# A fixed order for the last token tile, and its output stored in two halves

## The chip, the cores and the metric

The kernel runs on one core of a Trainium2 chip. The core has a matrix engine (TensorE, PE in the profile, with its weight loads under PEld), a vector engine (VectorE, DVE), an activation engine (ScalarE, ACT), GpSimd (POOL) and a sync engine (SyncE, SP) that here only starts transfers. The engines run beside one another, each in its own order, and wait for one another by semaphores. The metric is the device time of one execution in microseconds; the kernel before has a median of 182.74 us in 4 runs (181.94 to 183.9).

## The reference

The computation is attention over 8 heads with a local window of 96 positions and 8 global ones, and behind it a mixing block whose input is the attention's output. With batch 4, sequence 768, model width 512:

```
x  = attention(q, k, v)                    # (4, 768, 512)
theta = x @ w_theta
zr, zi = x * cos(theta), x * sin(theta)
y  = w_tok_r @ zr + w_tok_i @ zi           # over the 768 positions
u  = x + y
out = u + max(u @ w_ch, 0)
```

The change touches only the last two lines, for the last 128 positions of the last batch.

## The kernel before, in words

Positions are cut into NT = 6 tiles of T = 128. Each of the 4 batches goes through three stages.

**Attention** (`prep`, `scores`, `values`) leaves x in `x_sb`. **theta** makes the angles, their cosine and sine, and the products `zri`. **The mixing block**, which is what matters here, has three steps for a tile `tt`:

- `mix(b, tt, g)`, g = 0 to 2: four matmuls each (L377), 12 in all, that add up y for the tile in one PSUM buffer. Behind the last one VectorE adds x and writes `u` (L382).
- `utrans(b, tt)`: turns `u` into `uT`, with the channels on the partitions. In batches 1 to 3 that is a transfer with transpose on SP's queue (L391), except for the very last tile, (3, 5). That one is turned by four TensorE transposes (L395) and a copy out of PSUM on ScalarE (L396).
- `chan(b, tt)`: four matmuls of `uT` with `w_ch` (L402), the activation and sum on VectorE into `o_sb` (L405), and a store of 256 KB on SP's queue (L407).

The program emits the steps of a batch in a list, `main`, and `chan` lags three tiles behind `mix`. In the last batch there is no further attention to weave in, so the list itself is what is emitted. Its end for tiles 4 and 5 is: mix(4,0), chan(1), mix(4,1), mix(4,2), utrans(4), mix(5,0), chan(2), mix(5,1), mix(5,2), utrans(5). The three `chan` steps that are left over, 3 to 5, are in `rest` (L565) and are emitted behind the loop (L568). The first part of the program has an order written out by hand (`manual_schedule`, L83, closed at L528); what follows it is ordered by the scheduler of the language, bound to lie behind the last instruction of that part on PE, DVE and ACT (`fences`). For the end of the last batch the built program's order on PE is the order of emission.

Small PSUM tiles (`ps`) come from a pool of four, taken in turn by `mix`, `utrans` and `chan`; `uT` has 5 buffers, `u` 6 and `o_sb` 4.

Of the kernel before, what the change touches and what calls it, by code (L numbers as in the profile page):

```python
# [12 lines left out]
ALU = mybir.AluOpType  # L13
# [3 lines left out]
def kernel(  # L17
# [13 lines left out]
    nc = tc.nc  # L31
    B, H, S, D = q.shape
    T = 128
    NT = S // T
    DM = H * D
# [20 lines left out]
    def ps_small(shape, dtype):  # L56
        return small.tile(shape, dtype, name="ps", tag="ps")
# [30 lines left out]
    for i_, eng in ((1, nc.sync), (0, nc.scalar)):  # L88
        eng.dma_start(out=qk32[:, i_].rearrange("p h t d -> p h (t d)"),
                      in_=(q, k)[i_][0, 0:2].rearrange("h (p t) d -> p h (t d)", p=T))  # L90
# [62 lines left out]
    def trans_w(tt, copy=nc.vector.tensor_copy):  # L153
        for wi in range(2):
            ps = ps_small([T, NT, T], BF)
            for st in range(NT):
                nc.tensor.transpose(ps[:, st, :], w_nat[wi, tt][:, st * T:(st + 1) * T], ident)
            (copy if wi else nc.vector.tensor_copy)(out=w_tokT[wi][:, :, tt * T:(tt + 1) * T], in_=ps)  # L158
# [50 lines left out]
    def prep(b, p):  # L209
        qk = loads[b][0]  # L210
        if (b, 0) not in qkT:
            alloc_x(b)

        qkn = att.tile([T, NT, 2, 2, D], BF, name="qkn", bufs=3)
        with behind("dve"):
            for i_ in range(2):
                nc.vector.tensor_copy(  # L217
                    out=qkn[:, :, i_].rearrange("p t h d -> p h t d"), in_=qk[:, i_, 2 * p:2 * p + 2])
        qT = att.tile([T, S], BF, name="qT", bufs=6)
        kT = att.tile([T, S], BF, name="kT", bufs=6)  # L220
        for i_, dst in ((0, qT), (1, kT)):
            ps = ps_small([T, NT, T], BF)
            with behind("pe"):
                for t_ in range(NT):
                    nc.tensor.transpose(ps[:, t_, :], qkn[:, t_, i_].rearrange("p h d -> p (h d)"), ident)  # L225

            dst = dst.rearrange("p (n t) -> p n t", t=NT)
            src = ps.rearrange("p t n -> p n t")
            if i_ == 0:
                nc.vector.tensor_copy(out=dst, in_=src)  # L230
            else:
                nc.scalar.copy(out=dst, in_=src)  # L232

        qkT[(b, p)] = [qT, kT, None]
        kglob(b, p)
# [113 lines left out]
    def theta(b, c, j):  # L349
        if c == 0 and j == 0:  # L350
            zri[b] = moe.tile([T, 2, NT, DM], BF, name="zri", tag="zri", bufs=1)
        xT, xb = xT_sb[b], x_sb[b]
        if j == 0:
            pss["th"] = ps_big()
        pb = pss["th"]
        st = 2 * c + j
        for dc in range(NC):
            nc.tensor.matmul(pb[:, j, :], lhsT=xT[:, dc, st * T:(st + 1) * T],  # L358
                             rhs=w_theta_bf[:, dc, :], start=(dc == 0), stop=(dc == NC - 1))
        if j == 1:  # L360
            cs = moe.tile([T, 2, 2, DM], BF, name="cs")
            nc.scalar.activation(cs[:, 0], pb, AF.Sin, bias=halfpi)  # L362
            ins = nc.scalar.activation(cs[:, 1], pb, AF.Sin).ins  # L363
            for i_ in range(2):
                for j_ in range(2):
                    nc.vector.tensor_mul(  # L366
                        zri[b][:, i_, 2 * c + j_, :].rearrange("p (g d) -> p g d", g=NP),
                        xb[:, :, 2 * c + j_, :],
                        cs[:, i_, j_].rearrange("p (g d) -> p g d", g=NP))

    def mix(b, tt, g):
        if g == 0:
            pss["mix"] = ps_small([T, DM], FP)
        ps = pss["mix"]
        for st in (2 * g, 2 * g + 1):
            for wi in range(2):
                anchor["pe"] = nc.tensor.matmul(  # L377
                    ps, lhsT=w_tokT[wi][:, st, tt * T:(tt + 1) * T], rhs=zri[b][:, wi, st, :],
                    start=(st == 0 and wi == 0), stop=(st == NT - 1 and wi == 1)).ins
        if g == NT // 2 - 1:  # L380
            u_sb[b, tt] = moe.tile([T, DM], BF, name="u", bufs=6)
            anchor["dve"] = nc.vector.tensor_add(  # L382
                u_sb[b, tt].rearrange("p (g d) -> p g d", g=NP), x_sb[b][:, :, tt, :],
                ps.rearrange("p (g d) -> p g d", g=NP)).ins

    def utrans(b, tt):
        u = u_sb[b, tt]
        uT = moe.tile([T, NC, T], BF, name="uT", bufs=5)
        uTs[(b, tt)] = uT
        if b and (b, tt) != (B - 1, NT - 1):  # L390
            nc.sync.dma_start_transpose(out=uT, in_=u)  # L391
            return
        ps = ps_small([T, NC, T], BF)
        for dc in range(NC):
            nc.tensor.transpose(ps[:, dc, :], u[:, dc * T:(dc + 1) * T], ident)  # L395
        nc.scalar.copy(out=uT, in_=ps)  # L396

    def chan(b, tt):
        u, uT = u_sb[b, tt], uTs[(b, tt)]
        ps_c = ps_small([T, DM], FP)  # L400
        for dc in range(NC):
            nc.tensor.matmul(ps_c, lhsT=uT[:, dc, :], rhs=w_ch_bf[:, dc, :],  # L402
                             start=(dc == 0), stop=(dc == NC - 1))
        o_sb = moe.tile([T, DM], FP, name="o_sb", bufs=4)
        nc.vector.scalar_tensor_tensor(o_sb, in0=ps_c, scalar=0.0, in1=u,  # L405
                                       op0=ALU.max, op1=ALU.add)
        nc.sync.dma_start(out=out[b, tt * T:(tt + 1) * T, :], in_=o_sb)  # L407

    def load_all(b):
        alloc_loads(b)  # L410
        load_qk(b, 0, 8)
        load_v(b, 0, 8)
# [4 lines left out]
    def load_piece(b, i):  # L417
        if i == 0:
            alloc_loads(b)
        g = nc.gpsimd.tensor_copy(out=gates[:, i:i + 1], in_=uTs[b - 2, i][0:1, 0, 0:1]).ins  # L420
        with tc.issue_after(g):
            if i < H // 2:
                load_qk(b, 2 * i, 2)
            else:
                load_v(b, (i - H // 2) * (H // 2), H // 2)
# [17 lines left out]
    def weave(main, side, s0=0.0, s1=1.0):  # L443

        total = float(sum(w for w, _ in main)) or 1.0
        stot = float(sum(w for w, _ in side)) or 1.0
        done, sdone, i_ = 0.0, 0.0, 0
        for w, f in main:
            f()
            done += w  # L450
            while i_ < len(side) and s0 + (s1 - s0) * (sdone + side[i_][0] / 2) / stot <= done / total:
                side[i_][1]()
                sdone += side[i_][0]
                i_ += 1
        while i_ < len(side):
            side[i_][1]()
            i_ += 1
# [74 lines left out]
    rest = []  # L532
    for b in range(B):
        nxt = b + 1 if b + 1 < B else None
        if b == 0:
            load_all(2)
        lag = 3
        th = [lambda c=c, j=j: theta(b, c, j) for c in range(NT // 2) for j in range(2)]
        pre = [lambda p=p: prep(nxt, p) for p in range(NP)] if nxt else []
        if b == 0:  # L540
            order = []
        elif nxt:
            order = rest[:-1] + pre[:2] + th[:2] + pre[2:] + th[2:3] + rest[-1:] + th[3:]
        else:
            order = rest[:-1] + th[:3] + rest[-1:] + th[3:]
        for f in order:
            f()
        main = []
        for tt in range(NT):
            for g in range(NT // 2):  # L550
                main.append((2048, lambda tt=tt, g=g: mix(b, tt, g)))
                if b == 0 and g == 1 and tt + 1 < NT:
                    main.append((1536, lambda tt=tt: trans_w(tt + 1)))
                if tt >= lag and g == 0:
                    main.append((2048, lambda tt=tt: chan(b, tt - lag)))
                if b == 0 and tt and g == 1:
                    main.append((512, lambda tt=tt: utrans(b, tt - 1)))
            if b:
                main.append((0, lambda tt=tt: utrans(b, tt)))
            if b == 1 and b + 2 < B:  # L560
                main.append((0, lambda tt=tt: load_piece(b + 2, tt)))
        side = [(1536, f) for f in pre] if b == 0 else []
        side += attention_steps(nxt) if nxt else []
        weave(main, side, 0.3 if b == 0 else 0.0, 0.9)
        rest = [lambda tt=tt, b=b: chan(b, tt) for tt in range(NT - lag, NT)]  # L565
        if b == 0:
            rest.insert(1, lambda b=b: utrans(b, NT - 1))
    for f in rest:  # L568
        f()
    fences.close()  # L570


# [33 lines left out]
```

## Time and profile before

| | |
|---|---|
| median of 4 runs | 182.74 us (181.94 to 183.9) |
| profiled execution | 183.61 us |
| its span, from the first to the last instruction | 181.7 us |
| PE busy | 164.3 us, 90% of the span |
| DVE busy | 134.8 us, 74% |
| ACT busy | 101.0 us, 56% |
| POOL busy | 31.5 us, 17% |
| output stores, all on SP's queue | 24 of 256 KB, median 2.4 us from issue to landing |

Times in the profile's views count from the start of the span. The profiled execution took 1.91 us more than its span, which lies outside the first and the last instruction. A row of the timeline names the start, the length, the engine, the line, the operation with its output and input, how many instructions are merged in it, and in brackets how long the engine had been idle and who ended that. PE's matmuls are pipelined: a row's length reaches to the modelled end of its last matmul, and the next matmul can start before that.

### The profile page before, as it was taken

The numbers are of one execution on the slowest core, as the hardware profiler recorded it, in microseconds if no ns is written. First come the engines' busy times: TensorE is split into PE (matmuls) and PEld (weight loads), VectorE is DVE, ScalarE is ACT, GpSimd is POOL, SyncE is SP. The second block draws the span as 40 slices with busy tenths as digits, with TensorE's granted clock in tenths as the row PEclk, the third lists the DMA queues.
The fourth block names the chain that finished last, engine by engine and source line by source line (L and its number), as shares of the span: only waits on it lengthen the run. The fifth ranks groups of instructions, "written<-read, shape, count | busy, mean of one in ns | idle before, by whom it ended". The sixth has DMA issues, their size and how long they took to land. (4 is left out here: it accounts for less than half of the span.)

```text
span 181.7 us, 3710 instructions
## 1 busy us (share of the span) xinstructions
PE 164.3 (90%) x1504; PEld 87.2 (48%) x1530; DVE 134.8 (74%) x299; ACT 101.0 (56%) x120; POOL 31.5 (17%) x43
## 2 busy tenths in 40 slices
PE   6789979999799999999999996998999999999981
PEld 1446564556555565543554642653554644444430
DVE  7578964769999998998867886798767874734342
ACT  2489776997776554789646401699645505700010
POOL 8974440040120000000424060300000000000000
PEclk9999999999999999999999997899999999999998
DMA  5999999999999927110399999991153385123334
GB/s 167 177 193 188 209 209 207 203 193 147 128 145 227 153 83 196 58 46 14 60 160 125 185 182 175 192 87 58 32 101 101 90 134 186 58 46 101 89 87 173
DMA packets 58193, 24.36 MB, mean 134 GB/s; under 512 B 44352, under 2 KB 55104, under 8 KB 58176
## 3 DMA queue, kind: packets, MB, share of 16 engines
q0 software_dynamic: 35328, 12.45, 78.3%
q1 hardware_dynamic: 22576, 11.28, 27.5%
q10 hardware_dynamic: 272, 0.39, 0.6%
q8 instruction: 12, 0.20, 0.4%
q14 instruction: 5, 0.04, 0.1%
HBM read 25.69 MB, written 6.29 MB: 176 GB/s over the span
## 5 line engine op out<-in xcount | busy, mean ns | idle before, releaser
L377 PE MATMUL ps<-zri,w_tokT 128*128 128x512 bf16 x273 | 68.9, 380 | 2.0 <-DVE zri L366 0.8
L273 ACT ACTIVATE e<-pb 128x1024 bf16<-128x1024 f32 (+1 forms) x48 | 43.0, 954 | 20.7 <-PE pb L266 20.5
L377 PEld LDWEIGHTS <-w_tokT 128*128 128x128 bf16 x288 | 26.2, 98 | 30.5 <-issue 2.1
L358 PE MATMUL pb<-w_theta_bf,xT 128*128 128x512 bf16 x91 | 23.7, 392 | 2.4 <-DMA xT<-x_sb 1.7
L382 DVE TENSOR_TENSOR u<-x_sb,ps 128x512 bf16<-128x512 bf16 x24 | 16.4, 684 | 11.3 <-PE ps L377 11.3
L366 DVE TENSOR_TENSOR zri<-x_sb,cs 128x512 bf16<-128x512 bf16 x48 | 18.3, 421 | 7.1 <-ACT cs L362 6.3
L402 PE MATMUL ps<-w_ch_bf,uT 128*128 128x512 bf16 x93 | 23.4, 379 | 0.2
L405 DVE SCALAR_TENSOR_TENSOR o_sb<-ps,u 128x512 f32<-128x512 f32 x24 | 16.4, 684 | 5.2 <-PE ps L402 5.2
L362 ACT ACTIVATE cs<-pb,halfpi 128x1024 bf16<-128x1024 f32 x12 | 13.4, 1118 | 11.5 <-issue 8.1
L232 ACT COPY kT<-ps 128x768 bf16<-128x768 bf16 x12 | 9.7, 807 | 16.5 <-PE ps L225 16.3
L283 DVE TENSOR_TENSOR e<-e,etab 128x1024 bf16<-128x1024 bf16 (+1 forms) x24 | 14.8, 619 | 3.7 <-ACT e L273 3.6
L266 PE MATMUL pb<-qT,kT 64*128 64x128 bf16 x224 | 16.0, 223 | 1.4 <-ACT e L273 0.6
L266 PEld LDWEIGHTS <-kT 64*128 64x128 bf16 x224 | 8.9, 95 | 16.1 <-issue 14.0
L396 ACT COPY uT<-ps 128x512 bf16<-128x512 bf16 x7 | 4.1, 580 | 21.6 <-PE ps L395 21.6
L358 PEld LDWEIGHTS <-xT 128*128 128x128 bf16 x96 | 9.0, 100 | 12.8 <-DMA xT<-x_sb 2.6
L323 PEld LDWEIGHTS <-e 128*128 128x128 bf16 x352 | 12.7, 97 | 2.9 <-issue 0.6
L230 DVE COPY qT<-ps 128x768 bf16<-128x768 bf16 x12 | 11.4, 948 | 2.9 <-PE ps L225 2.9
L225 PE MATMUL ps<-ident,qkn 128*128 128x128 bf16 x144 | 11.4, 228 | 1.8 <-DVE qkn L217 1.7
L402 PEld LDWEIGHTS <-uT 128*128 128x128 bf16 x96 | 8.6, 98 | 8.9 <-DMA uT<-u 0.4
L78 POOL DMA_DIRECT2D vn<-in_v_dram x6 | 10.2, 1699 | 13.1 <-DVE w_tokT L158 11.4
L225 PEld LDWEIGHTS <-qkn 128*128 128x128 bf16 x144 | 9.3, 102 | 6.5 <-DVE qkn L217 4.9
L363 ACT ACTIVATE cs<-pb 128x1024 bf16<-128x1024 f32 x12 | 12.3, 1023 | 0.0
(69 smaller groups left out, 196.1 us busy)
## 6 DMA issues: line engine op xcount, KB each, us to landing
out_dram<-o_sb SPq DMA_DIRECT2D x24, 256.0 KB, 2.4
vn<-in_v_dram POOLq DMA_DIRECT2D x4, 384.0 KB, 8.9
qk<-in_q_dram POOLq DMA_DIRECT2D x2, 768.0 KB, 13.1
qk<-in_k_dram POOLq DMA_DIRECT2D x2, 768.0 KB, 15.8
vn<-in_v_dram POOLq DMA_DIRECT2D x2, 768.0 KB, 20.9
qk<-in_q_dram POOLq DMA_DIRECT2D x7, 192.0 KB, 4.8
qk<-in_k_dram POOLq DMA_DIRECT2D x7, 192.0 KB, 5.5
w_nat<-in_moe_w_tok_r_dram POOLq DMA_DIRECT2D x3, 384.0 KB, 13.6
```

Source lines behind the costliest of these rows:

```text
L225: nc.tensor.transpose(ps[:, t_, :], qkn[:, t_, i_].rearrange("p h d -> p (h d)"), ident)
L266: nc.tensor.matmul(pb[:, hh, o:o + T], lhsT=lhsT, rhs=qT[R, (own, nxt)[part]], start=bool(b), stop=bool(b) or (jt == NT - 1 or (j == 1 and ...
L273: ins = nc.scalar.activation(e_c, pb[:, :, 0:n], AF.Exp, scale=scale).ins
L283: nc.vector.tensor_mul(e_c, e_c, tab[:, :, s0:s0 + n // T].rearrange("p a s n -> p a (s n)"))
L323: nc.tensor.matmul(o, lhsT=l_, rhs=r_, start=(i_ == 0), stop=(i_ == len(mms) - 1))
L358: nc.tensor.matmul(pb[:, j, :], lhsT=xT[:, dc, st * T:(st + 1) * T], rhs=w_theta_bf[:, dc, :], start=(dc == 0), stop=(dc == NC - 1))
L362: nc.scalar.activation(cs[:, 0], pb, AF.Sin, bias=halfpi)
L366: nc.vector.tensor_mul(zri[b][:, i_, 2 * c + j_, :].rearrange("p (g d) -> p g d", g=NP), xb[:, :, 2 * c + j_, :], cs[:, i_, j_].rearrange( ...
L377: anchor["pe"] = nc.tensor.matmul(ps, lhsT=w_tokT[wi][:, st, tt * T:(tt + 1) * T], rhs=zri[b][:, wi, st, :], start=(st == 0 and wi == 0), ...
L382: anchor["dve"] = nc.vector.tensor_add(u_sb[b, tt].rearrange("p (g d) -> p g d", g=NP), x_sb[b][:, :, tt, :], ps.rearrange("p (g d) -> p g ...
L402: nc.tensor.matmul(ps_c, lhsT=uT[:, dc, :], rhs=w_ch_bf[:, dc, :], start=(dc == 0), stop=(dc == NC - 1))
L405: nc.vector.scalar_tensor_tensor(o_sb, in0=ps_c, scalar=0.0, in1=u, op0=ALU.max, op1=ALU.add)
```

## The change

`chan` writes the output of the last tile in two halves of 256 channels. Each half has its own VectorE instruction and its own store; the first store goes to SP's queue and the second to ACT's. All other tiles stay as they were.

For tile 5 of the last batch, `mix`, `utrans` and the `chan` step of tile 2 are taken out of the list. In their place a block at the end writes the order for PE and DVE by hand: chan(2), then the 12 matmuls of tile 5, chan(3), the transposes of tile 5, chan(4), chan(5). The same instructions run on PE as before. In the built program PE's order differs only within the last 40 matmuls; DVE's order differs only in the one instruction that became two; ACT has one more instruction, the store, behind its last copy; SP's last store has half the size, and SP's order is the same.

```diff
@@ chan @@
         o_sb = moe.tile([T, DM], FP, name="o_sb", bufs=4)
-        nc.vector.scalar_tensor_tensor(o_sb, in0=ps_c, scalar=0.0, in1=u,
-                                       op0=ALU.max, op1=ALU.add)
-        nc.sync.dma_start(out=out[b, tt * T:(tt + 1) * T, :], in_=o_sb)
+        parts = 2 if (b, tt) == (B - 1, NT - 1) else 1
+        for i_ in range(parts):
+            cols = slice(i_ * DM // parts, (i_ + 1) * DM // parts)
+            nc.vector.scalar_tensor_tensor(o_sb[:, cols], in0=ps_c[:, cols], scalar=0.0, in1=u[:, cols],
+                                           op0=ALU.max, op1=ALU.add)
+            (nc.scalar if i_ else nc.sync).dma_start(
+                out=out[b, tt * T:(tt + 1) * T, cols], in_=o_sb[:, cols])
@@ main list @@
-                main.append((2048, lambda tt=tt, g=g: mix(b, tt, g)))
+                if (b, tt) != (B - 1, NT - 1):
+                    main.append((2048, lambda tt=tt, g=g: mix(b, tt, g)))
...
-                if tt >= lag and g == 0:
+                if tt >= lag and g == 0 and (b, tt) != (B - 1, NT - 1):
                     main.append((2048, lambda tt=tt: chan(b, tt - lag)))
...
-            if b:
+            if b and (b, tt) != (B - 1, NT - 1):
                 main.append((0, lambda tt=tt: utrans(b, tt)))
@@ behind the loop @@
-    for f in rest:
-        f()
+    with tc.manual_schedule(engines={mybir.EngineType.PE, mybir.EngineType.DVE}):
+        chan(B - 1, NT - 4)
+        for g in range(NT // 2):
+            mix(B - 1, NT - 1, g)
+        chan(B - 1, NT - 3)
+        utrans(B - 1, NT - 1)
+        chan(B - 1, NT - 2)
+        chan(B - 1, NT - 1)
     fences.close()
```

## The prediction

> **What bounds the kernel now.** I read the page's busy shares first: PE is busy for 90% of the span, so time can only be had where PE stands still or after its last matmul. The chain of work that ended last, from 170 us on, shows both places (start, length, what):
>
> ```profile
> 169.83 1.73 PE ps L377 x8
> 171.55 0.86 PE ps L402 x4
> 172.42 1.74 PE ps L377 x8
> 174.16 0.02 issue
> 174.18 0.70 DVE u L382
> 174.88 0.05 issue
> 174.93 0.40 PE ps L395 x4
> 175.32 2.60 PE ps L402 x12
> 177.93 0.02 issue
> 177.95 0.69 DVE o_sb L405
> ```
>
> PE works without a break until tile 5's mix ends at 174.16. Then the chain leaves it for the addition on VectorE (0.70), comes back for the transposes, and PE still has the 12 matmuls of chan(3), chan(4) and chan(5) to do. Eight of these need nothing of tile 5. The timeline of that stretch shows who waits:
>
> ```profile
> 172.25 1.89 PE L377 MATMUL ps<-zri,w_tokT 128*128 128x512 bf16 x8
> 174.18 0.69 DVE L382 TENSOR_TENSOR u<-x_sb,ps 128x512 bf16<-128x512 bf16 x1 [1.04 <-PE ps L377]
> 174.93 0.40 PE L395 MATMUL ps<-ident,u 128*128 128x128 bf16 x4 [0.78 <-DVE u L382]
> 175.16 2.75 PE L402 MATMUL ps<-w_ch_bf,uT 128*128 128x512 bf16 x12
> 175.41 0.59 ACT L396 COPY uT<-ps 128x512 bf16<-128x512 bf16 x1 [17.47 <-PE ps L395]
> 177.95 0.69 DVE L405 SCALAR_TENSOR_TENSOR o_sb<-ps,u 128x512 f32<-128x512 f32 x1 [0.17 <-PE ps L402]
> 178.67 0.33 SPq L407 DMA_DIRECT2D out_dram<-o_sb  x1
> ```
>
> The copy of uT ends at 176.00, but chan(5), which wants it, starts only behind eight matmuls. From the transfers' view between 178 and 182 us I read the last piece (40 slices of 0.1 us):
>
> ```profile
> DMA  9999614999999606999899200000000000000000
> out_dram<-o_sb SPq DMA_DIRECT2D x2, 256.0 KB, 2.0
> ```
>
> The last store is issued at 178.67, moves bytes from about 179.5 to 180.25, and lands 2.0 us after its issue, at 180.67. So 0.83 pass before the first byte, 0.75 in motion, 0.42 to the landing; then 1.03 to the end of the span at 181.7.
>
> **Part 1: chan(3) into PE's gap.** Twelve matmuls take 2.75 with a modelled 0.379 for the last, so the pitch is (2.75 - 0.379)/11 = 0.216 and a chan block takes 0.86 of PE. The last mix matmul starts at 173.76, so chan(3) can start at 173.98 and its last slot ends at 174.84. The transposes still wait for u and start at 174.93 as before: chan(3) fits into the gap and delays nothing. chan(4) takes the place that chan(3) had, 175.16, and leaves PE free at 176.02. chan(5) then needs the copy: 176.00 plus the 0.05 that u takes to reach PE, 176.05. Before, it started at 175.16 + 8 x 0.216 = 176.89. **The gain is 0.84**, and its last matmul ends at 177.07 instead of 177.91.
>
> What is late next is the copy on ScalarE: the cover of chan(4) is 0.03 too short, so a later copy costs its full lateness. The hand-over is bounded by 0 and by the 0.08 seen from the transposes to the copy (175.33 to 175.41), which makes the gain 0.81 to 0.86.
>
> chan(3) and chan(4) must have their inputs. The transposing transfers of u(3) and u(4) start on SP at 167.99 and 171.44 and land in 2.4 and 2.5, at 170.4 and 173.94; they are wanted at 173.98 and 175.16, with 3.6 and 1.2 to spare. The PSUM buffers of the new turn (chan(3) takes mix(4)'s, the transposes chan(1)'s, chan(4) chan(2)'s, chan(5) mix(5)'s) were all read by 174.87.
>
> **Part 2: chan(2) ahead of tile 5's mix.** It swaps 0.86 of PE work with four mix matmuls, of the same sum; u(5) keeps its time. Its uT was issued at 164.54, six microseconds before it is wanted at 170.5. Its output on VectorE comes at about 171.6 instead of 172.46, behind u(4), and its store waits for SP to finish the 1.20 of u(4)'s transfer at 172.64, 0.5 earlier than now. Its bytes then start at 173.47 and may run beside the last half microsecond of u(4)'s transfer; that would cost at most 0.5 of the 1.2 to spare. I take nothing. Removing that cover entirely would cost what it is late, since chan(4) stands ahead of chan(5) on PE.
>
> **Part 3: two halves on VectorE.** No half-sized row of this instruction exists. The nearest are two instructions that read f32 from PSUM: 128x384 in 557 ns and 128x768 in 957, a slope of 1.04 ns per column and 157 fixed; that gives 690 for 512 (the row has 690) and 424 for 256. The Trainium skill, page "VectorE: DVE Perf Modes", section on the TRN2 errata, speaks against splitting: a fixed latency is paid for each instruction, (N + 151)/0.96 ns. By that rule two halves take 848, 0.16 more than one. The row of two equally long instructions in one stretch says less:
>
> ```profile
> 157.05 0.76 DVE L366 TENSOR_TENSOR zri<-x_sb,cs 128x512 bf16<-128x512 bf16 x2 [0.24 <-ACT cs L362]
> ```
>
> One of these takes 421, yet two take 0.76, so the second starts before the first ends. It reads SBUF, but has the length of a half; I take 0.76 and keep 0.85 as the other end. VectorE starts at 177.09, the first half ends at 177.51, the second at 177.85 (before: 178.64).
>
> **Part 4: two stores on two queues.** SP issues the first half at 177.54; ACT, idle since its copy, the second at 177.88, with nothing queued behind it. The store of chan(4) is issued at 176.95 and moves bytes from 177.78 to 178.53. The first half's bytes could start at 178.37 and follow it to 178.90; the second's could start at 178.71 and end with the queue at 179.28. Landing 0.42 later is 179.70, and the span ends at 180.73. Before, 3.79 lay between the end of chan(5)'s last matmul and the end of the span (181.7 - 177.91); now it is 3.66 (180.73 - 177.07), another 0.13.
>
> The page "DMA: Bandwidth & Descriptors" of the Trainium skill, sections "Anatomy of one DMA" and "Issuing engines are not separate DMA queues", says that a transfer pays about 2.0 us whatever its size, plus bytes/436e9, and that a second issuing engine saves only issue time. By that (a fit for GpSimd's transfers) a 128 KB half would need 2.3, land at 180.18, and the total gain would be 0.49. The measured 2.0 for twice the bytes contradicts so high a constant, so I take the trace. Two things stay unknown. The 1 KB pieces could take as long as the 2 KB pieces do now: then both halves move for 1.5 instead of 0.75, and the gain falls by 0.75. And ACT's queue has one row only, at 0.73 us: issue 0.47 against SP's 0.46 there, landing 4.6 against SP's 4.2 for an equal load beside it. I add nothing for it and keep 0.4 as the other end. From below, no row suggests that ACT is quicker than SP's 2.0.
>
> **The sum.** 0.84 + 0.13 = 0.97. The profiled span goes from 181.7 to 180.73, with its 1.91 outside to 182.64. That execution stood 0.87 above the median of 182.74, so I forecast 182.74 - 0.97 = 181.8.
>
> **The rivals.**
>
> *The halves give back what they cost* (chance 0.24). The gap is closed, but VectorE's 0.09, half of ACT's 0.4 and half of the 0.75 for small pieces come off, 0.67: the total gain is 0.3, the time 182.4. For it: no row shows a 1 KB store or ACT's queue late in the run. Against it: SP's stores flow at over 300 GB/s in the last slices and nothing else uses the engines.
>
> *The wait moves* (0.08). PE's gap is filled, but the chain u, transposes, copy, chan(5) has only chan(4) as cover; if the copy comes 0.5 later, 0.34 of the 0.84 stays, with 0.13 from the stores: time 182.3. Against it: ACT has been idle for 17.47 when the transposes come, and nothing is ahead of the copy.
>
> *Slower: ACT's queue is cold* (0.06). If its store, the first since 0.73 us, lands as that first one did, 4.6 after its issue, it lands at 182.5 and the span ends at 183.5, 1.8 longer: 184.5. It decides from a landing of 2.8 on (180.67 - 177.88). Against it: that row was a 384 KB load beside GpSimd's loads, and SP's took 4.2 there and 2.0 at the end.
>
> *The change does not do what it says* is excluded by the built order: PE has chan(3) ahead of the transposes, and ACT has the store.
>
> **How the numbers follow.** The forecast has 0.62. The first three cases lie between 181.8 and 182.4; with every unknown at its dear end (0.09, 0.4, 0.75) the time is 183.0. The four runs of before spread by 1.96, so that a median of a few can be off by about half a microsecond to a whole one. The range is therefore 180.9 to 182.9. One per cent, 1.83 us, is about what a measurement of this kernel can tell from no change. Over 1% faster needs twice the gap and would be drift, 0.08; slower by over 1% needs the cold queue at its full price or drift, 0.04; within, 0.88.
>
> **What the changed profile would show.** No idle row at the transposes longer than 0.1; PE's L402 rows split 4, 4, 4 with the last starting about 0.83 earlier; the copy ending within 0.1 of chan(5)'s start; two VectorE rows of about 424 ns; ACT's store landing within about 1.8 of its issue; the span 1.0 shorter. I am wrong if the transposes start later than 174.93 relative to the mix, if chan(5) waits for the copy by more than 0.1, or if the last store lands more than 2.3 after its issue.

## The result, and the profile after

The changed kernel takes 182.13 us (median of 44 runs) against 183.13 us (63 runs) for the kernel before, measured beside it: a ratio of 0.9939, 95% interval 0.9922 to 0.9956. That is 1.1 us (0.8 to 1.4), 0.6%; the forecast was 0.97 us and a time of 181.8. The ratio leaves out executions that took over 1.5% longer than the fastest of the same kernel; two of the profiles below (one more store, seven cut stores) are of such executions, and in both the tail, as it is defined next, ran at the full clock.

The profiled execution has a span of 179.2 us, 2.5 less than the one before. Not all of that is the change. The addition of tile 4 on VectorE comes from matmuls ahead of everything that was moved, and it already starts 1.45 us earlier in this execution (169.28 against 170.73). What follows it I call the **tail**: from the start of that addition to the end of the span. Before, it took 10.95; now it takes 9.88. The change is worth 1.07 there. These are the windows of the two tails (start and end, length, then busy time of PE, PEld, DVE, ACT and POOL, granted clock, transfers' share, GB/s):

```profile
170.73:181.68 10.95, 6.40 (x32) 2.69 (x30) 4.14 (x6) 0.59 (x1) 0.00 (x0) 0.92 0.37 126
169.28:179.16 9.88, 6.35 (x32) 2.61 (x30) 4.20 (x7) 0.59 (x1) 0.00 (x0) 1.00 0.42 139
```

The 0.92 of the kernel before comes from a clock that fell at 179.97, behind PE's last matmul. The expectations below were written with spans read to 0.1, so they speak of 10.97 and 9.92; tails and landings in the text are from the kept traces, to 0.01.

The chain of work that ended last, of the changed kernel (start, length, what):

```profile
170.10 2.59 PE ps L377 x12
172.69 0.86 PE ps L402 x4
173.56 0.32 PE ps L395 x4
173.87 1.77 PE ps L402 x8
175.65 0.02 issue
175.67 0.42 DVE o_sb L408
176.09 0.33 DVEq L612
```

VectorE's addition of u is gone from the middle of the chain. PE goes from tile 5's mix to chan(3), to the transposes and to the last eight matmuls. The timeline of the same stretch shows what each step waited for (start, length, engine, line, operation; in brackets idle time and who ended it):

```profile
172.53 1.03 PE L402 MATMUL ps<-w_ch_bf,uT 128*128 128x512 bf16 x4
172.73 0.69 DVE L382 TENSOR_TENSOR u<-x_sb,ps 128x512 bf16<-128x512 bf16 x1 [1.90 <-PE ps L377]
173.48 0.40 PE L395 MATMUL ps<-ident,u 128*128 128x128 bf16 x4
173.71 1.92 PE L402 MATMUL ps<-w_ch_bf,uT 128*128 128x512 bf16 x8
173.96 0.59 ACT L396 COPY uT<-ps 128x512 bf16<-128x512 bf16 x1 [17.47 <-PE ps L395]
174.59 0.55 PEld L402 LDWEIGHTS <-uT 128*128 128x128 bf16 x4 [0.35 <-ACT uT L396]
175.67 0.76 DVE L408 SCALAR_TENSOR_TENSOR o_sb<-ps,u 128x256 f32<-128x256 f32 x2 [0.21 <-PE ps L402]
176.46 0.36 ACTq L410 DMA_DIRECT2D out_dram<-o_sb  x1
```

The transposes have no idle time any more, and they start 4.20 after tile 4's addition, as before. Eight matmuls at the pitch of 0.216 would take 1.89; the row has 1.92, so chan(5) waits 0.03 for the copy on ScalarE. VectorE starts on chan(5) 6.39 after tile 4's addition instead of 7.22. The transfers in the last 4 us (40 slices of 0.1 us; below, stores with size and time to landing):

```profile
DMA  9999993000059999999999999820000000000000
out_dram<-o_sb SPq DMA_DIRECT2D x1, 256.0 KB, 2.0
out_dram<-o_sb SPq DMA_DIRECT2D x1, 128.0 KB, 1.8
out_dram<-o_sb ACTq DMA_DIRECT2D x1, 128.0 KB, 1.8
```

The store of chan(4) and the two halves move without a break from 176.3 to 177.9. The last half is issued at 176.46 and lands at 178.27, 8.99 after tile 4's addition; before, the last landing came 9.97 after it.

### The profile page after: what moved, and what is told of

The parts are those of the page before. It is cut to its first block, busy times and chain, and to the rows that moved or that the text cites. A ratio compares the mean times of both kernels' runs of the same rounds, so it can differ in the third digit from the quotient of the medians.

```text
span 179.2 us, 3714 instructions
## 1 busy us (share of the span) xinstructions
PE 162.4 (91%) x1504; PEld 86.2 (48%) x1530; DVE 134.5 (75%) x300; ACT 101.2 (56%) x120; POOL 32.0 (18%) x43
## 5 line engine op out<-in xcount | busy, mean ns | idle before, releaser
L358 PE MATMUL pb<-w_theta_bf,xT 128*128 128x512 bf16 x91 | 22.6, 379 | 1.5 <-DMA xT<-x_sb 0.7
L408 DVE SCALAR_TENSOR_TENSOR o_sb<-ps,u 128x512 f32<-128x512 f32 (+1 forms) x25 | 16.5, 663 | 3.8 <-PE ps L402 3.8
L266 PE MATMUL pb<-qT,kG 64*128 64x128 bf16 x128 | 11.8, 216 | 0.3 <-DVE kG L207 0.3
L225 PE MATMUL ps<-ident,qkn 128*128 128x128 bf16 x144 | 10.6, 220 | 1.4 <-DVE qkn L217 1.2
L333 DVE TENSOR_TENSOR x_sb<-pb,rec 128x768 bf16<-128x768 f32 x12 | 11.5, 957 | 0.4
```

Source lines behind the costliest of these rows:

```text
L266: nc.tensor.matmul(pb[:, hh, o:o + T], lhsT=lhsT, rhs=qT[R, (own, nxt)[part]], start=bool(b), stop=bool(b) or (jt == NT - 1 or (j == 1 and ...
L408: nc.vector.scalar_tensor_tensor(o_sb[:, cols], in0=ps_c[:, cols], scalar=0.0, in1=u[:, cols], op0=ALU.max, op1=ALU.add)
```

## The experiments

The whole time of one kernel differs by three microseconds and more from its quickest run to its slowest, so I read the tail, and the ratio to the kernel before where there were enough runs. Each tail is of one profiled execution. First, how far the tail itself can be trusted.

**The two kernels once more.**

> The kernel before once more, to see how far the tail differs from one profile to the next. Theory: the tail is set by waits and fixed durations and is 10.97 within 0.06, while the span itself may differ by a microsecond or two. Rival: the tail differs by 0.2 or more, and readings of it under that mean nothing.

> The changed kernel once more, for the same reason: tail 9.92 within 0.06; rival: 0.2 or more away.

Measured: 10.94 and 9.91. The tail repeats within 0.03, and the landing of the last store (9.97 and 8.99 after tile 4's addition) to 0.01, while the start of the tail moved by half a microsecond in both.

**The order alone** (e1_order_only).

```diff
-        parts = 2 if (b, tt) == (B - 1, NT - 1) else 1
+        parts = 1
```

> The fixed order alone; tile 5's output is added and stored whole, on SP's queue. I read the tail: from the start of tile 4's addition (the last u row but one on VectorE) to the end of the span; it is 10.97 us in the kernel before and 9.92 in the changed one. Theory (0.84 of the gain is PE's gap, 0.13 the halves): tail 10.13, and about 0.45% faster than before. Rival (the halves carry the gain, the order only moves the wait): tail above 10.6.

Measured: tail 10.07, ratio 0.9934 (0.9899 to 0.9969). Of the 1.07, the order brings 0.88. Its timeline has the transposes without idle time, and VectorE's last addition, as in the changed kernel, 6.39 after tile 4's:

```profile
169.86 0.69 DVE L382 TENSOR_TENSOR u<-x_sb,ps 128x512 bf16<-128x512 bf16 x1 [1.03 <-PE ps L377]
174.06 0.40 PE L395 MATMUL ps<-ident,u 128*128 128x128 bf16 x4
176.25 0.69 DVE L408 SCALAR_TENSOR_TENSOR o_sb<-ps,u 128x512 f32<-128x512 f32 x1 [0.20 <-PE ps L402]
```

**The halves alone** (e2_halves_only). `chan` as in the changed kernel, everything behind it as before.

> The two halves alone, on two queues, in the order of the kernel before. Theory: PE's gap stays (0.78 idle at the transposes), the store lands 0.1 to 0.2 earlier than before: tail 10.75 to 10.87, within 0.15% of before. Rival (the halves carry the gain): tail below 10.4.

Measured: tail 10.78, ratio 0.9969 (0.9939 to 0.9998). By the tail the halves bring 0.17 here and 0.16 to 0.19 on top of the order (10.07 against 9.91 and 9.88). The ratio's interval holds that too. Its timeline shows PE's gap untouched:

```profile
174.62 0.40 PE L395 MATMUL ps<-ident,u 128*128 128x128 bf16 x4 [0.78 <-DVE u L382]
177.65 0.75 DVE L408 SCALAR_TENSOR_TENSOR o_sb<-ps,u 128x256 f32<-128x256 f32 x2 [0.17 <-PE ps L402]
```

The two parts add up. The rival that the halves carry the gain has fallen.

**Both halves on SP's queue** (e3_halves_sp).

```diff
-            (nc.scalar if i_ else nc.sync).dma_start(
+            nc.sync.dma_start(
```

> As the changed kernel, but both halves are stored on SP's queue. Theory (the second half is ready only 0.34 after the first, and SP's issue takes 0.33, so that ACT's queue saves nothing): tail 9.92 within 0.06. Rival (two queues are what helps): tail above 10.1, with the second store issued over 0.15 after its half is ready.

Measured: tail 9.97, with the landing at 9.06 instead of 8.99 after tile 4's addition. The second queue does not save nothing, as the theory had it, but 0.07. The second half is ready at 177.53, and SP starts on it 0.12 later, where ACT started 0.03 after its half was ready:

```profile
177.65 0.40 SPq L410 DMA_DIRECT2D out_dram<-o_sb  x1
```

The theory was right in that the saving is small. But the halves as a whole bring the landing only 0.13 forward behind the new order (9.12 to 8.99), so about half of that comes from the second queue, by this one run.

**chan(4) ahead of the transposes too** (e4_both_ahead).

```diff
         chan(B - 1, NT - 3)
-        utrans(B - 1, NT - 1)
         chan(B - 1, NT - 2)
+        utrans(B - 1, NT - 1)
         chan(B - 1, NT - 1)
```

> As the changed kernel, but chan(4) too stands ahead of the transposes, so that nothing covers the copy on ScalarE. Theory (one block covers the addition, the other must cover the copy): PE idles some 0.7 ahead of chan(5), chan(5) starts 0.77 later than in the changed kernel, tail 10.7, little better than before. Rival (it is enough to fill the gap at the addition): tail 9.9.

Measured: tail 10.62, ratio 0.9965 (0.9939 to 0.9992). The gap at the addition is filled twice over, but the copy is uncovered, and in its timeline PE stands still in another place:

```profile
176.19 0.58 ACT L396 COPY uT<-ps 128x512 bf16<-128x512 bf16 x1 [18.24 <-PE ps L395]
176.83 1.04 PE L402 MATMUL ps<-w_ch_bf,uT 128*128 128x512 bf16 x4 [0.72 <-ACT uT L396]
```

One block has to lie on each side of the transposes. That was the working behind the 0.84, and it decides.

**The copy twice** (e5_copy_twice). ScalarE copies the same PSUM tile into uT two times.

> As the changed kernel, but ScalarE copies tile 5's uT out of PSUM twice, one after the other, which makes it about 0.55 later; the result is the same. Theory (the copy ends with no slack ahead of chan(5)): chan(5) waits the whole of it, tail 10.4 to 10.5. Rival (the copy has slack behind chan(4)): tail 9.9 to 10.1.

Measured: tail 10.47. The two copies take 1.20 instead of 0.59, and VectorE's start on chan(5) moves by the same 0.61, from 6.39 to 7.00 after tile 4's addition. In its timeline PE stands idle ahead of chan(5):

```profile
173.52 1.20 ACT L397 COPY uT<-ps 128x512 bf16<-128x512 bf16 x2 [17.47 <-PE ps L395]
174.78 1.04 PE L403 MATMUL ps<-w_ch_bf,uT 128*128 128x512 bf16 x4 [0.47 <-ACT uT L397]
```

So the copy is next in line, with no slack, as the 0.03 of wait says.

**chan(2) back in its old place** (e6_chan2_back).

```diff
-        chan(B - 1, NT - 4)
         for g in range(NT // 2):
             mix(B - 1, NT - 1, g)
+            if g == 0:
+                chan(B - 1, NT - 4)
```

> As the changed kernel, but chan(2) is back between the first four and the last eight mix matmuls of tile 5. Theory (this move is of the same PE work and nothing waits for it): tail 9.92 within 0.06. Rival (the early chan(2) relieves VectorE or SP's queue at the end): tail longer by 0.15 or more.

Measured: tail 9.90. That move is worth nothing, in either direction.

**Is there more to have at the end?** (e7_chan5_cols). VectorE waits for all of chan(5) before it starts the first half. I cut the matmuls too.

```diff
-        ps_c = ps_small([T, DM], FP)
-        for dc in range(NC):
-            nc.tensor.matmul(ps_c, lhsT=uT[:, dc, :], rhs=w_ch_bf[:, dc, :],
...
         for i_ in range(parts):
             cols = slice(i_ * DM // parts, (i_ + 1) * DM // parts)
+            ps_c = ps_small([T, DM // parts], FP)
+            for dc in range(NC):
+                nc.tensor.matmul(ps_c, lhsT=uT[:, dc, :], rhs=w_ch_bf[:, dc, cols],
+                                 start=(dc == 0), stop=(dc == NC - 1))
...
```

> As the changed kernel, but chan(5)'s matmuls too run in two halves of 256 columns, with a PSUM buffer each, so that VectorE can take the first half while PE does the second. VectorE ends 0.34 earlier. Theory A (the bytes of chan(4)'s store stand ahead in the transfer engines and bound the end): tail 9.8 to 9.9. Theory B (VectorE's two halves bound the end): tail 9.6.

Measured: tail 9.97, not better than 9.88 or 9.91. VectorE ends 6.85 after tile 4's addition instead of 7.15, but the last store, issued 0.3 earlier, takes 2.1 to its landing instead of 1.8, and lands 8.99 after tile 4's addition in both kernels. That fits theory A for the landing: the bytes ahead of it bound the end. The tail was even 0.07 over the expectation, for which I had no reason yet.

With chan(4) cut in the same way and stored in halves (e8_chan45_cols; parts is 2 for both tiles):

> As e7_chan5_cols, and chan(4) in two column halves and two stores as well, so that its bytes start about 0.7 earlier. Theory A: now the end of VectorE bounds it, tail 9.5 to 9.6, and about 0.8% faster than before. Theory B: the same tail as in e7_chan5_cols.

Measured: tail 9.93, ratio 0.9952 (0.9926 to 0.9979). Theory A missed by 0.4. Theory B's number came, but not for its reason: the landing did come earlier, as theory A had it. The last store was issued at 177.21 and landed 1.73 later, at 178.94, which is 8.59 after tile 4's addition against 8.99. But from there the span took another 1.35 to its end, where the changed kernel takes 0.89. What SP does in between stands in its rows at the end of the program; EVENT_SEMAPHORE is a wait for a semaphore. This is the changed kernel's row, from 178.2 on (line, engine, operation, count, duration in ns least/median/most, first and last start):

```profile
L612 SPq EVENT_SEMAPHORE  x1: 28/28/28, 178.3 to 178.3; - x1
```

And this is the same row of this kernel, from 178.9 on:

```profile
L612 SPq EVENT_SEMAPHORE  x8: 27/28/28, 179.0 to 179.4; - x8
```

At the end SP waits for the semaphores of the transfers one after the other. The eight here start within 0.43, so they are 0.061 apart. Transfers from SP and ACT take eight semaphores in turn. In the changed kernel, with 56 such transfers, the last store has the last one in SP's list, and the other waits are over when it lands. With 57, the last store has the first one, and the seven other waits run behind its landing. (With chan(5) alone in column halves, the half that landed last had the seventh, and one more wait ran behind its landing, which goes with its 0.07 too much.) This is a theory that can be tried from both sides.

**Shift the turn away from the changed kernel** (e10_one_more_store). One store in the middle of the run is cut into two:

```diff
...
+            cuts = 2 if (b, tt) == (1, 0) else 1
+            for j_ in range(cuts):
+                w = (cols.stop - cols.start) // cuts
+                cc = slice(cols.start + j_ * w, cols.start + (j_ + 1) * w)
+                eng.dma_start(out=out[b, tt * T:(tt + 1) * T, cc], in_=o_sb[:, cc])
```

> As the changed kernel, with one change far from its end: the store of batch 1's first tile is cut into two on SP's queue, so that the last store falls on the semaphore that is waited for first. Theory (turn of the semaphores): the landing comes as in the changed kernel, and the tail grows from 9.92 to about 10.35, at best 0.35% faster than before. Rival: tail 9.92, as a store in the middle of the run cannot matter at the end.

Measured: tail 10.31, ratio 0.9986 (0.9955 to 1.0017). The last store is issued at 178.81 and lands 1.81 later, at 180.62, which is 8.99 after tile 4's addition, to the hundredth that of the changed kernel. Then the waits follow, in SP's row from 180.55 on:

```profile
L616 SPq EVENT_SEMAPHORE  x8: 27/28/28, 180.6 to 181.1; - x8
```

A store cut in batch 1 costs 0.40 to 0.43 at the end of the program (10.31 against 9.91 and 9.88); seven waits of 0.061 are 0.43.

**Shift it back for the column halves** (e9_cols_last_wait). The same cut for seven stores, so that the turn comes round:

```diff
+            cuts = 2 if b == 1 or (b, tt) == (2, 0) else 1
```

> As e8_chan45_cols, and seven earlier stores (all six tiles of batch 1 and the first of batch 2) are cut into two on SP's queue, so that the last store again falls on the last of the eight transfer semaphores in their turn. Theory (in e8 the last store fell on the semaphore that SP waits for first at the end, and eight more waits of about 0.055 each ran behind its landing): those waits lie ahead of the landing again, tail 9.95 - 0.45 = 9.5, about 0.8% faster than before. Rival (the landing itself was late, or the column halves bring nothing): tail 9.9 to 10.0.

Measured: tail 9.51, as forecast, 0.37 to 0.40 under the changed kernel's. With 64 transfers the last store's own wait is the last again, as SP's row from 180.2 on shows:

```profile
L616 SPq EVENT_SEMAPHORE  x1: 28/28/28, 180.3 to 180.3; - x1
```

The whole time does not show it, though: the ratio is 0.9973 (0.995 to 0.9997), where the tail alone would give 1 - 1.44/183 = 0.992. Something ahead of the tail took about a microsecond back. In its profile tile 4's addition starts at 171.73, and in that of the one cut store at 171.63, against 169.79 for the changed kernel in the same series. The granted clock fell in both around 125 us; these are the windows of the kernel with seven cut stores (PE and PEld busy, DVE, ACT, POOL, then granted clock, transfers' share, GB/s):

```profile
125.00:130.00 5.00, 5.00 (x40) 1.77 (x39) 2.92 (x6) 2.19 (x3) 0.00 (x0) 0.74 0.14 26
170.00:181.00 11.00, 8.09 (x48) 4.17 (x46) 5.15 (x9) 0.59 (x1) 0.00 (x0) 1.00 0.47 144
```

The tail ran at the full clock, so its reading stands. Whether the cut stores make such a dip more frequent was not tried; they are not needed for one, since the profile of the kernel before has one too. Nor does the dip account for what is missing. The 11 runs of this version with a mean clock of 0.998 or more have a median of 181.80 against 182.28 for 27 such runs of the kernel before: 0.48 less (0.1 to 0.9 by resampling these runs), where the tail gives 1.44. What else was lost ahead of the tail stays open. I do not call this version faster than the changed kernel.

Landings count from the start of tile 4's addition; a row without a ratio is of one run.

| kernel | tail, us | last landing, us | ratio to before |
|---|---|---|---|
| before, and again | 10.95, 10.94 | 9.97, 9.97 | 1 |
| changed, and again | 9.88, 9.91 | 8.99, 8.99 | 0.9939 (0.9922 to 0.9956) |
| order alone | 10.07 | 9.12 | 0.9934 (0.9899 to 0.9969) |
| halves alone | 10.78 | 9.87 | 0.9969 (0.9939 to 0.9998) |
| both halves on SP | 9.97 | 9.06 | |
| chan(4) ahead of the transposes too | 10.62 | 9.70 | 0.9965 (0.9939 to 0.9992) |
| copy twice | 10.47 | 9.56 | |
| chan(2) back | 9.90 | 8.99 | |
| chan(5) in column halves | 9.97 | 8.99 | |
| chan(4) and chan(5) in column halves | 9.93 | 8.59 | 0.9952 (0.9926 to 0.9979) |
| the same, turn of semaphores restored | 9.51 | 8.60 | 0.9973 (0.995 to 0.9997) |
| changed, turn shifted by one store | 10.31 | 8.99 | 0.9986 (0.9955 to 1.0017) |

## Why the prediction was right

**Part 1, chan(3) in the gap (0.84).** Right in its size and in its working. VectorE's start on chan(5) moved from 7.22 to 6.39 after tile 4's addition, 0.83. The transposes did not move, and the wait for the copy is the 0.03 that was worked out. Two runs show that both covers are needed: without the one on the copy 0.74 of the gain is lost, and with a copy 0.61 longer VectorE starts 0.61 later and the tail grows by 0.56 to 0.59. The rival that the wait moves named the right place, but the copy was not late.

**Part 2, chan(2).** Taken at nothing, and it is nothing (9.90 without, 9.88 and 9.91 with).

**Part 3, the halves on VectorE.** The two take 0.76, the value taken from the row with two instructions of that length, not the 0.85 that was estimated from the page "VectorE: DVE Perf Modes" of the Trainium skill (section on the TRN2 errata). Each alone has about the length that the rule gives, 423 and 414 ns against 424, but the second starts 0.34 after the first, before that one ends. In the run with column halves in chan(4) and chan(5) the four halves start 0.44 to 0.46 apart (175.42, 175.86, 176.32, 176.75). That says nothing of VectorE: each follows its own four matmuls, and PE makes those in 0.44 (the 16 of both tiles take 1.93).

**Part 4, the stores (0.13).** The halves brought the landing forward by 0.13 behind the new order (9.12 to 8.99) and by 0.10 in the old one (9.97 to 9.87). The landing after ACT's issue was forecast at 179.70 - 177.88 = 1.82 and was 1.81. The 1 KB pieces do not move at half the rate: chan(4)'s store and the halves, 512 KB, pass in 1.6 us without a break, where 256 KB took 0.75. So the rival of dear halves and that of a cold queue on ACT both fall. The rule of the page "DMA: Bandwidth & Descriptors" of the Trainium skill (section "Issuing engines are not separate DMA queues") that a second issuing engine saves only issue time is borne out: ACT started 0.09 sooner than SP could, and the landing came 0.07 sooner. The page's fit for GpSimd's transfers (section "Anatomy of one DMA"), from which 2.3 was estimated, does not carry over to these: 1.81 in all is less than its fixed part of 2.0 alone.

**The sum (0.97).** The landing came 0.98 earlier, from 9.97 to 8.99. The tail fell by more, 1.03 to 1.07, and the rest is at the end. The time from landing to end was carried over unchanged; it was 0.98 before and is 0.89 and 0.92 in the two profiles of the changed kernel. In the kernel before, with 55 transfers, the store that landed last was the last but one in SP's list, and one more wait of 0.06 ran behind the landing, as SP's row from 180.69 on shows; in the changed kernel it is the last:

```profile
L601 SPq EVENT_SEMAPHORE  x2: 28/28/28, 180.7 to 180.8; - x2
```

The remaining 0.03 is no more than the tail of one kernel differs. The time of 181.8 was built on the 182.74 of four runs; on the 183.13 measured beside the changed kernel, the same 0.97 gives 182.16, against 182.13 measured. And the prediction held one per cent to be about the least that a measurement can tell, where 0.6% stands clear of nothing here.

**What was not foreseen** is that adding a transfer at all turns the semaphores. The change adds one, and that happened to be the favourable direction by one wait. That was luck: the run with one more shows that the same cut could have cost some 0.4 of the gain. No row of the forecast spoke of it.

## What to carry to other kernels

Behind the last matmuls that depend on a chain through other engines, put one independent block at each wait of that chain (here one behind the addition and one behind the transposes), and compare its length with the wait; a block too many at one wait uncovers the other. Before a store is split over two queues, compare the time between the pieces with the time that one queue needs from issue to issue (here 0.34 against 0.43, worth 0.07). In a kernel of which only the end is changed, measure the stretch from the last untouched step to the end: here it repeats to 0.03 us where the whole run differs by several microseconds.

## What I had not expected of the hardware

- The end of the program has an order of its own. SP's waits for the transfers' semaphores take 0.061 each, and how many of them run behind the last landing depends on how many transfers the program has issued before: 0.40 to 0.43 in the kernel with one more store, and 0.42 between the two versions with column halves (9.93 and 9.51).
- A wait of PE in the middle of the run is sometimes followed by a lower granted clock, and sometimes not. These rows are of the same matmuls behind the same wait, in the kernel before and in the second profile of the changed kernel:

```profile
111.87 1.46 PE L358 MATMUL pb<-w_theta_bf,xT 128*128 128x512 bf16 x3 [1.70 <-DMA xT<-x_sb]
112.47 1.04 PE L358 MATMUL pb<-w_theta_bf,xT 128*128 128x512 bf16 x4 [2.31 <-DMA xT<-x_sb]
```

  In the first, PE was idle for 1.70 and the granted clock from 110 to 115 was 0.67; in the second PE was idle for 2.31 and the clock there stayed at 1.00. Beside the run of the order alone, 16 of the 48 runs of the kernel before that its ratio rests on have a mean clock under 0.9925; their median is 183.84, that of the others 182.56. So a lower clock goes with 1.3 us more, about the size of the 1.45 by which the first two profiles differ ahead of the tail. That it is the cause of that difference, and what sets it off, is not shown.
